# Second MoE from its second group of tokens on: seven half-size products and their sums in place of eight

## The chip, the cores and the metric

The kernel runs on one core of a Trainium2 chip. The core has five engines that run side by side, each with its own queue of instructions, taken in order: PE (TensorE, the matrix products), DVE (VectorE), ACT (ScalarE), POOL (GpSimd) and SP, which issues most transfers. The metric is the device time of one execution in microseconds (us), as the median of several runs; lower is better.

## The reference, cut to what matters

```python
attn_out = _attn_ref(**attn_kwargs)              # 4 x 8 heads, 576 positions, 64 wide
x = ...reshape(B * S, H * D)                     # 2304 tokens x 512
x = _moe_ref(x=x, **moe_kwargs)                  # first MoE: 512 -> 1024 -> 512
return _moe2_ref(x=x, **moe2_kwargs)             # second MoE

def _moe2_ref(x, w_gate, w_val, w_out):          # 512 -> 1536 -> 512
    gate = 1.0 / (1.0 + np.exp(-(x @ w_gate)))
    val = x @ w_val
    return (gate * val @ w_out).astype(np.float32)
```

The change is in the two products `x @ w_gate` and `x @ w_val` alone.

## The kernel before

Every float32 or float64 operand is held as two float16 parts, a high part and the remainder (low). A product of two such operands is three products on PE: high by high, high by low, low by high, summed in float32 in PSUM, the memory that PE writes. It has eight banks of 512 float32 columns.

The kernel first does the attention with the first MoE beside it. The first MoE's result, scaled and split in two parts, goes to a scratch in HBM (`x2_d`, 18 blocks of 128 tokens). The second MoE then takes the tokens in five groups: groups 0 to 3 of 512 tokens (four blocks), group 4 of 256.

For a group, the loop `for j in range(12)` makes 128 columns of the hidden 1536 at a time (L1134): 12 matmuls for the gate and 12 for the value, each 128 x 128 weights by 512 token columns (256 in group 4). Then ACT takes the sigmoid (L1139), DVE multiplies it by the value (L1140), ACT rounds the result to float16 (L1142) and DVE makes the low part (L1143). After that comes the product with `w_out`, called `ops` (L1150): 36 matmuls of 512 columns for each block of 128 tokens, and ACT takes the result out (L1154).

The weights of the second MoE come in as float64 words. The list `units` holds their preparation in 76 steps: `w2_dec` makes a float32 of them (`decode`, L166 on ACT, then L167, L168, L171 on DVE), `w2_scale` and `w2_scale_out` work out scales, `w2_split` cuts a piece into the two parts in `split_w`: POOL scales it (L639), ACT rounds it (L642), POOL subtracts (L643). The steps that are left when the second MoE begins are taken during group 0, some for each `j`; the last are `w2_scale_out`, a chain of small DVE instructions that ends with the scale `S_O` (L1066), and the twelve pieces of `w_out`, which POOL can only begin once `S_O` is there.

The order on each engine is not that of the code: a scheduler that reckons with expected durations sets it when the program is built. On the chip each engine then takes its instructions in that fixed order, so one that waits holds up all behind it.

Of the kernel before, what the change touches and what calls it, by code (L numbers as in the profile page):

```python
# [86 lines left out]
def attn_moe_kernel(  # L87
# [45 lines left out]

    def pow2(st, cols, dst, sdst, p=None):
# [914 lines left out]
    def w2_scale(jc):  # L1049
        pow2(w2st, [(4 * jc, 4 * jc + 4)], sw[:, jc, P_G:P_G + 1], sw[:, jc, S_G:S_G + 1], psx[0])  # L1050
# [5 lines left out]
        root2(mx, 1, sw[:, jc, P_L:P_L + 1], sw[:, jc, S_L:S_L + 1])  # L1056
        dve.scalar_tensor_tensor(out=sw[:, jc, W_CG:W_CG + 1], in0=col(P_F), scalar=2.0 ** -23,
                                 in1=sw[:, jc, P_G:P_G + 1], op0=ALU.mult, op1=ALU.mult)
# [51 lines left out]
    grow("gv", NGV, ctx, "left")  # L1110
    ob_p = enter(ctx, "ob", 2)
    for g in range(5):
        n = 4 if g < 4 else 2
# [4 lines left out]
        gvs = []
        for j in range(12):
# [18 lines left out]
            sg = ring("sg", [128, 512], F32)
            act.activation(out=sg[:, 0:nn], in_=prods[0], func=ACTF.Sigmoid, scale=sw[:, j // 4, W_CG:W_CG + 1])  # L1139
            dve.scalar_tensor_tensor(out=sg[:, 0:nn], in0=prods[1], scalar=2.0 ** -16, in1=sg[:, 0:nn],  # L1140
                                     op0=ALU.mult, op1=ALU.mult)
            act.activation(out=gv[:, 0, jj, 0:nn], in_=sg[:, 0:nn], func=ACTF.Copy)  # L1142
            dve.tensor_tensor(out=gv[:, 1, jj, 0:nn], in0=sg[:, 0:nn], in1=gv[:, 0, jj, 0:nn], op=ALU.subtract)  # L1143
# [88 lines left out]
```

## Time and profile before

| what | value |
|---|---|
| median of 3 runs | 1145.22 us (1144.88 to 1147.71) |
| span of the profiled execution, first to last instruction | 1146.8 us |
| PE busy | 990.4 us, 86% of the span |
| DVE busy | 721.4 us, 63% |
| ACT busy | 561.8 us, 49% |
| POOL busy | 405.2 us, 35% |
| mean granted TensorE clock | 0.882 of full speed |

A span is cut into slices or windows, and each engine's busy time in one is given. Busy shares are means over stages with different limits, so they are read stage by stage. The span stands in for the profiled execution's time; it lies within the three runs.

### The profile page before, as it was taken

The numbers are of one execution on the slowest core, as the hardware profiler recorded it, in microseconds if no ns is written. First come the engines' busy times: TensorE is split into PE (matmuls) and PEld (weight loads), VectorE is DVE, ScalarE is ACT, GpSimd is POOL, SyncE is SP. The second block draws the span as 40 slices with busy tenths as digits, with TensorE's granted clock in tenths as the row PEclk, the third lists the DMA queues.
The fourth block names the chain that finished last, engine by engine and source line by source line (L and its number), as shares of the span: only waits on it lengthen the run. The fifth ranks groups of instructions, "written<-read, shape, count | busy, mean of one in ns | idle before, by whom it ended". The sixth has DMA issues, their size and how long they took to land.

```text
span 1146.8 us, 21879 instructions
## 1 busy us (share of the span) xinstructions
PE 990.4 (86%) x8686; PEld 584.7 (51%) x8686; DVE 721.4 (63%) x1537; ACT 561.8 (49%) x1072; POOL 405.2 (35%) x349
## 2 busy tenths in 40 slices
PE   3535665877999889999999989879999999999998
PEld 3433343544555565666677666434444444444475
DVE  7899999799679788967965798892022022022021
ACT  5856567643567565746664567664222122122122
POOL 2556546632355553653555076646100000000000
PEclk9555565565988899999999999999999999999999
DMA  9879999785899998999987523551001100100000
GB/s 303 281 166 252 196 213 246 170 186 149 214 191 192 211 194 221 174 175 232 201 150 162 169 102 129 188 180 37 38 1 37 37 1 2 45 10 1 19 20 19
DMA packets 287863, 158.03 MB, mean 138 GB/s; under 512 B 233104, under 2 KB 258064, under 8 KB 287760
## 3 DMA queue, kind: packets, MB, share of 16 engines
q1 hardware_dynamic: 286736, 155.58, 57.2%
q8 instruction: 68, 1.11, 0.4%
q0 software_dynamic: 1024, 1.05, 0.3%
q14 instruction: 35, 0.29, 0.1%
HBM read 81.75 MB, written 20.05 MB: 89 GB/s over the span
## 4 chain that ended last, share of the span: by engine, by line
PE 42%; DVE 8%; DMA 5%; issue 2%; ACT 2%; POOL 1%; SPq 0%; ACTq 0%; POOLq 0%; DVEq 0%
PE s_ps L1134 20%; PE ops L1150 12%; PE xps L572 2%; PE x2ps L765 2%; DVE w2f L168 2%; DMA pt<-p 2%; PE hps L706 2%; DMA wraw<-in_moe_w_gate_dram 1%; DVE w2f L171 1%; DVE w2f L167 1%; DVE e L731 1%; DMA wraw<-in_moe_w_out_dram 1%; DMA wraw<-in_moe_w_val_dram 1%; PE s_ps L492 1%; POOL p L549 1%
## 5 line engine op out<-in xcount | busy, mean ns | idle before, releaser
L1134 PE MATMUL s_ps<-xb,w2f 128*128 128x512 f16 (+1 forms) x1440 | 291.3, 360 | 8.9 <-DVE sg L1140 5.3
L1134 PEld LDWEIGHTS <-w2f 128*128 128x128 f16 x1440 | 141.4, 99 | 152.0 <-issue 12.4
L549 POOL TENSOR_TENSOR p<-p,p 128x1024 f16<-128x1024 f32 x72 | 158.2, 2197 | 129.7 <-ACT p L548 87.1
L1140 DVE SCALAR_TENSOR_TENSOR sg<-s_ps,sg 128x512 f32<-128x512 f32 (+1 forms) x60 | 38.2, 637 | 261.2 <-ACT sg L1139 261.1
L537 ACT ACTIVATE p<-p,m,sc 128x576 f32<-128x576 f32 x144 | 123.4, 859 | 74.3 <-DVE m L535 66.4
L572 PE MATMUL xps<-gk,pt 128*128 128x64 f16 (+1 forms) x2240 | 132.8, 207 | 15.2 <-DVE xt L628 6.4
L1150 PE MATMUL ops<-w2f,gv 128*128 128x512 f16 x648 | 144.3, 379 | 0.0
L765 PE MATMUL x2ps<-lt,w1f 128*128 128x128 f16 x1728 | 124.7, 222 | 10.1 <-DVE lt L754 7.2
L572 PEld LDWEIGHTS <-pt 128*128 128x128 f16 (+1 forms) x2240 | 106.6, 108 | 45.8 <-issue 20.5
L765 PEld LDWEIGHTS <-w1f 128*128 128x128 f16 x1728 | 105.7, 99 | 30.5 <-issue 19.1
L530 DVE CUSTOM_DVE_ANT_0 p<-s_ps,gk 128x576 f32<-128x576 f32 x144 | 106.2, 750 | 22.8 <-PE s_ps L492 12.9
L1139 ACT ACTIVATE sg<-s_ps,sw 128x512 f32<-128x512 f32 (+1 forms) x60 | 38.5, 642 | 140.4 <-PE s_ps L1134 140.4
L398 PEld LDWEIGHTS <-mask 128*128 128x128 f16 (+1 forms) x1312 | 68.5, 126 | 73.9 <-DVE gb L423 23.8
L1150 PEld LDWEIGHTS <-gv 128*128 128x128 f16 x648 | 63.4, 98 | 75.2
L489 PE MATMUL s_ps<-gk,qt 128*128 128x288 f16 x256 | 61.9, 326 | 28.6 <-DVE m L530 20.0
L398 PE MATMUL bp<-rhs,mask 128*128 128x64 f16 (+1 forms) x960 | 56.5, 234 | 32.7 <-DVE gb L423 22.3
L706 PE MATMUL hps<-w1f,xt 128*128 128x512 f16 x312 | 77.2, 395 | 0.0
L548 ACT ACTIVATE p<-p 128x1152 f16<-128x1152 f32 x54 | 62.4, 1156 | 24.2 <-DMA pt<-p 23.6
L492 PE MATMUL s_ps<-gk,qt 64*128 64x288 f16 x256 | 63.5, 327 | 0.0
L1154 ACT ACTIVATE ob<-ops,sc 128x512 f32<-128x512 f32 x18 | 12.3, 688 | 97.2 <-PE ops L1150 95.7
L1143 DVE TENSOR_TENSOR gv<-sg,gv 128x512 f16<-128x512 f32 (+1 forms) x60 | 38.7, 646 | 32.8 <-ACT gv L1142 32.8
L706 PEld LDWEIGHTS <-xt 128*128 128x128 f16 x384 | 36.9, 101 | 42.5 <-issue 8.1
(164 smaller groups left out, 1477.0 us busy)
## 6 DMA issues: line engine op xcount, KB each, us to landing
gk<-bias_d SPq DMA_DIRECT2D x24, 576.0 KB, 5.7
wraw<-in_moe_w_out_dram SPq DMA_DIRECT2D x20, 512.0 KB, 4.2
wraw<-in_moe_w_gate_dram SPq DMA_DIRECT2D x12, 512.0 KB, 4.0
wraw<-in_moe_w_val_dram SPq DMA_DIRECT2D x12, 512.0 KB, 4.0
sraw<-in_q_dram SPq DMA_DIRECT2D x12, 384.0 KB, 5.1
sraw<-in_k_dram SPq DMA_DIRECT2D x12, 384.0 KB, 4.1
sraw<-in_v_dram SPq DMA_DIRECT2D x12, 384.0 KB, 4.1
bias_d<-gk SPq DMA_DIRECT2D x8, 576.0 KB, 4.5
```

The source lines that it names most:

```text
L398: pe.matmul(big[0:np_, jj // 8, o:o + 64], lhsT, rhs[i].rearrange("p c h g -> p (c h g)"), start=(i == 0), stop=(i == 1),)
L489: pe.matmul(s_[:, n, 0:288], qt[:, 2 * hh + r, :], kt[:, o], start=True, stop=False)
L492: pe.matmul(s_[:, n, 0:288], qt[rows, 4 + r, :], kt[rows, o], start=False, stop=True)
L530: dve.tensor_tensor_reduce(out=pp[:, r].rearrange("p (i j) -> p i j", i=2), in0=ss[r][:, :, 0:288], in1=bi.rearrange("p (i j) -> p i j", i ...
L537: act.activation(out=pp[:, r], in_=pp[:, r], func=ACTF.Exp, bias=m[:, 2 + r:3 + r], scale=col(C), accum_out=sm[:, cs[r]:cs[r] + 1])
L548: act.activation(out=hi, in_=pp, func=ACTF.Copy)
L549: pool.tensor_tensor(out=p16[:, :, 640:1152], in0=pp[:, :, 0:512], in1=hi[:, :, 0:512], op=ALU.subtract)
L572: pe.matmul(o, a, b_, start=(n == 0), stop=(n == len(seq) - 1))
L706: pe.matmul(h, xt[:, xl, kk, off:off + 128], win16[:, 2 * kk + n, wl], start=(kk == 0 and xl == 0 and wl == 0), stop=(kk == 3 and xl == 1),)
L765: pe.matmul(ps[:, dc], wout16[:, f, wl, 128 * dc:128 * dc + 128], lt[:, ll, f], start=(n == 0), stop=(n == 23))
L1134: pe.matmul(ps[:, 0:n], w[:, 4 * (j // 4) + c, wl, o:o + 128], xx[:, 0:n, c, xl, :], start=(m == 0), stop=(m == 11))
L1150: pe.matmul(ps, gvs[j // 4][:, gl, j % 4, 128 * tt:128 * tt + 128], w2h16[2][:, j, wl], start=(m == 0), stop=(m == 35))
```

## The change

From group 1 on, the gate and the value product of 512 hidden columns (a chunk `jc`; there are three) are no longer made of eight products of halved operands (2 halves of the 512 inputs, 2 of the hidden columns, 2 of the tokens) but of seven, on sums and differences of the halves (the scheme of Strassen and Winograd). Group 0 stays as it was.

- `w2_sums` makes the sums of weight halves once for each of six matrices (gate and value, three chunks); `x2_sums` makes those of the tokens once for each group. A sum is made in float32 and split in two parts: 14 DVE and 4 ACT instructions for each call.
- `product` is one of the seven: 12 matmuls of 256 token columns (128 in group 4) into a PSUM bank. There are six banks for it, and two for `ops`.
- `seven` adds the seven products up: ACT copies the first one, DVE makes seven additions. `gate_val7` applies sigmoid, product and split to the four quarters that come out.

```diff
+    def add(out_, a, b, op=ALU.add):
+        dve.tensor_tensor(out=out_, in0=a, in1=b, op=op)
+    def split_sum(x, dst):
+        act.activation(out=dst(0), in_=x, func=ACTF.Copy)
+        add(dst(1), x, dst(0), ALU.subtract)
...
+    def w2_sums(mat, jc):
...
+        add(x, a11(0), a21(0), ALU.subtract)
+        add(u, a11(1), a21(1), ALU.subtract)
+        add(x, x, u)
+        split_sum(x, s3)
...
+        split_sum(u, a21)
...
+    def product(w, x, nn):
+        p = ps_b.tile([128, 2, 256], F32, name="prod", tag="prod")
+        for jf in range(2):
+            m = 0
+            for kk in range(2):
+                for (wl, xl) in ((0, 0), (0, 1), (1, 0)):
+                    pe.matmul(p[:, jf, 0:nn], w(wl, kk, jf), x(xl, kk), start=(m == 0), stop=(m == 5))
+                    m += 1
+        return p[:, :, 0:nn]
+    def seven(mat, jc, xs_, nn):
+        w = wsum[mat, jc]
+        a, b, c, d = (f32t()[:, :, 0:nn] for _ in range(4))
+        act.activation(out=a, in_=product(w["a11"], xs_["b11"], nn), func=ACTF.Copy)
+        add(b, product(w["s2"], xs_["t2"], nn), a)
+        add(a, product(w["a12"], xs_["b21"], nn), a)
+        add(c, product(w["s3"], xs_["t3"], nn), b)
+        p5 = product(w["s1"], xs_["t1"], nn)
+        add(b, p5, b)
+        add(d, p5, c)
+        add(c, product(w["a22"], xs_["t4"], nn), c)
+        add(b, product(w["s4"], xs_["b22"], nn), b)
...
+    load_x2(1)
+    gvs = []
+    gate_val(0, 4, xb.pop(0), gvs)
+    while units:
+        units.pop(0)()
...
+    for jc in range(3):
+        for mat in range(2):
+            w2_sums(mat, jc)
+        if jc == 0:
+            xs_ = x2_sums(1)
+    second_out(0, 4, gvs)
...
+    for g in range(1, 5):
+        n = 4 if g < 4 else 2
+        if g < 4:
+            load_x2(g + 1)
+        gvs = []
+        gate_val7(n, xs_, gvs)
+        if g < 4:
+            xs_ = x2_sums(g + 1)
+        second_out(g, n, gvs)
```

Besides, the scales of the gate and value weights are halved, so that sums fit float16, and some buffers get other places. Lines named below in rows of the changed kernel are its own: L1140 is `add`, L1143 the ACT half of `split_sum`, L1210 a matmul of `product`, L1218 the ACT copy in `seven`, L1278 `ops` (L1150 before), L1254 and L1122 the DVE instructions of group 0 (L1140 and L1143 before), L1253 and L1121 their ACT counterparts, L1071 the scale `S_O` (L1066 before), and L1282 ACT's copy of `ops` (L1154 before).

The first place is DVE at the end of the preparation of `w_out`: the small chain `L147` to `L1066` that ends with `S_O`. Before, these rows stand there, with one instruction of group 0 between them:

```order
L147 TENSOR_SCALAR cl<-tot 128x3
L149 TENSOR_SCALAR ci<-cl 128x3
L150 TENSOR_SCALAR ci<-ci 128x3
L151 TENSOR_SCALAR sw<-ci 128x3
L1143 TENSOR_TENSOR gv<-sg,gv 128x512
L153 RECIPROCAL rc<-sw 128x3
L1062 TENSOR_TENSOR sw<-sw 128x3
L1063 TENSOR_REDUCE sc<-sw 128x1
L1064 RECIPROCAL sc<-sc 128x1
L1066 SCALAR_TENSOR_TENSOR sw<-sw,sc 128x1 x3
```

In the changed kernel the end of the same chain (`L1068` to `L1071`) reads as follows, on DVE; `fr` are the float32 buffers, `w2f_...` weights, `w2s_...` split sums of weights, `xb` tokens:

```order
L1254 SCALAR_TENSOR_TENSOR fr<-s_ps,fr 128x512
L1140 TENSOR_TENSOR fr<-xb,fr 128x2x2x128
L1140 TENSOR_TENSOR fr<-xb 128x2x2x128
L1140 TENSOR_TENSOR w2s_11182<-fr,w2s_11182 128x512
L1068 TENSOR_REDUCE sc<-sw 128x1
L1140 TENSOR_TENSOR w2s_11207<-fr,w2s_11207 128x512
L1140 TENSOR_TENSOR fr<-w2f_9501 128x512
L1140 TENSOR_TENSOR fr<-fr,xb 128x2x2x128
L1122 TENSOR_TENSOR gv<-fr,gv 128x512
L1069 RECIPROCAL sc<-sc 128x1
L1140 TENSOR_TENSOR fr<-fr 128x512
L1071 SCALAR_TENSOR_TENSOR sw<-sw,sc 128x1 x3
```

Between the reduction `acc` (L140) that begins the chain and L1071 there stand 33 instructions of 512 elements on DVE in the changed kernel (27 sums and 6 of group 0), and three of group 0 before.

The second place is also on DVE, further on, where the sums end and the first products of group 1 (`prod`) are added:

```order
L1140 TENSOR_TENSOR w2f_9501<-fr,w2f_9501 128x2x256
L1140 TENSOR_TENSOR fr<-fr,w2f_9501 128x512
L1140 TENSOR_TENSOR w2s_11309<-fr,w2s_11309 128x512
L1140 TENSOR_TENSOR w2s_11334<-fr,w2s_11334 128x512
L1140 TENSOR_TENSOR fr<-w2f_9501,fr 128x512
L1140 TENSOR_TENSOR w2s_11334<-fr,w2s_11334 128x512
L1140 TENSOR_TENSOR fr<-prod,fr 128x512
L1140 TENSOR_TENSOR fr<-fr,w2f_9501 128x512
L1140 TENSOR_TENSOR fr<-prod,fr 128x512 x2
L1140 TENSOR_TENSOR w2s_11334<-fr,w2s_11334 128x512
L1140 TENSOR_TENSOR fr<-prod,fr 128x512 x7
```

From L1071 to the first row with `prod` there are 69 sums. All of them, those of the third chunk too, stand ahead of the first addition of a product.

The third place is ACT in the same stretch, where the copies of `ops` of group 0 (L1282) and the first copy of a product (L1218) stand between the ACT halves of the sums:

```order
L1143 ACTIVATE w2s_11284<-fr 128x512
L1282 ACTIVATE ob<-ops,sc 128x512 x3
L1143 ACTIVATE w2s_11284<-fr 128x512
L1143 ACTIVATE w2s_11309<-fr 128x512
L1143 ACTIVATE w2f_9500<-fr 128x2x256
L1282 ACTIVATE ob<-ops,sc 128x512
L1143 ACTIVATE w2s_11309<-fr 128x512
L1143 ACTIVATE w2f_9501<-fr 128x2x256
L1143 ACTIVATE w2s_11309<-fr 128x512
L1143 ACTIVATE w2s_11334<-fr 128x512 x2
L1218 ACTIVATE fr<-prod 128x512
```

Each L1143 waits for a sum on DVE, so the copies behind it come after that sum. On PE, the 144 matmuls of `ops` of group 0 stand in one piece, behind the last product of group 0 and ahead of all products of group 1; before, products of group 1 stood among them.

## Rows read from the trace of the kernel before

**Rows 1.** Page, part 1: busy time, share of the span, instructions of each engine.

```profile
PE 990.4 (86%) x8686; PEld 584.7 (51%) x8686; DVE 721.4 (63%) x1537; ACT 561.8 (49%) x1072; POOL 405.2 (35%) x349
```

**Rows 2.** Busy time in windows: length, engines, then PE clock, DMA share, GB/s.

```profile
764.00:786.00 22.00, 19.84 (x84) 8.68 (x85) 16.27 (x38) 12.37 (x27) 4.27 (x6) 0.92 0.23 73
786.00:823.00 37.00, 37.00 (x173) 16.84 (x172) 2.91 (x4) 10.21 (x17) 19.48 (x21) 1.00 0.14 50
880.00:1000.00 120.00, 120.00 (x558) 54.38 (x556) 18.00 (x26) 21.93 (x33) 0.00 (x0) 1.00 0.09 29
```

**Rows 3.** Chain that ended last: start, us, engine, tile, line, count.

```profile
842.72 10.36 PE s_ps L1134 x48
...
880.27 28.92 PE ops L1150 x134
...
1095.67 7.86 PE s_ps L1134 x72
...
1142.69 0.69 ACT ob L1154
```

**Rows 4.** Timeline of PE, first MoE: products of 128 columns in one run.

```profile
643.10 4.80 PE L765 MATMUL x2ps<-lt,w1f 128*128 128x128 f16 x83
```

**Rows 5.** Timeline of PE, end of group 0's gate and value products.

```profile
780.18 8.79 PE L1134 MATMUL s_ps<-xb,w2f 128*128 128x512 f16 x40
...
790.11 22.83 PE L1150 MATMUL ops<-w2f,gv 128*128 128x512 f16 x105
```

**Rows 6.** Timeline of DVE, group 0: decoding, then the chain to the scale.

```profile
768.92 0.41 DVE L167 TENSOR_SCALAR w2f<-w2f 128x512 int32<-128x512 int32 x1
769.25 0.68 DVE L171 SCALAR_TENSOR_TENSOR w2f<-wraw,w2f 128x512 int32<-128x512 int32 x1
769.85 0.68 DVE L168 SCALAR_TENSOR_TENSOR w2f<-wraw,w2f 128x512 int32<-128x512 int32 x1
770.57 0.69 DVE L171 SCALAR_TENSOR_TENSOR w2f<-wraw,w2f 128x512 int32<-128x512 int32 x1
...
777.31 0.16 DVE L140 TENSOR_REDUCE acc<-w2st 128x1 f32<-128x4 f32 x1 [0.25 <-ACT w2junk L1043]
...
782.96 0.30 DVE L1066 SCALAR_TENSOR_TENSOR sw<-sw,sc 128x1 f32<-128x1 f32 x3
```

**Rows 7.** Timeline of POOL: weight pieces beside a busy DVE, then beside an idle one.

```profile
735.14 3.00 POOL L639 TENSOR_SCALAR w2tmp<-w2f,sw 128x512 f32<-128x512 f32 x2
738.42 3.18 POOL L643 TENSOR_TENSOR w2f<-w2tmp,w2f 128x512 f16<-128x512 f32 x2 [0.27 <-ACT w2f L642]
...
783.29 1.36 POOL L639 TENSOR_SCALAR w2tmp<-w2f,sw 128x512 f32<-128x512 f32 x2 [17.65 <-DVE sw L1066]
784.73 2.27 POOL L643 TENSOR_TENSOR w2f<-w2tmp,w2f 128x512 f16<-128x512 f32 x2
```

**Rows 8.** Timeline of POOL and DVE where both are dense.

```profile
757.24 3.09 POOL L643 TENSOR_TENSOR w2f<-w2tmp,w2f 128x512 f16<-128x512 f32 x2 [1.23 <-ACT w2f L642]
757.66 0.68 DVE L1140 SCALAR_TENSOR_TENSOR sg<-s_ps,sg 128x512 f32<-128x512 f32 x1
...
760.31 2.48 POOL L639 TENSOR_SCALAR w2tmp<-w2f,sw 128x512 f32<-128x512 f32 x2
...
762.76 2.88 POOL L643 TENSOR_TENSOR w2f<-w2tmp,w2f 128x512 f16<-128x512 f32 x2
...
764.66 1.53 DVE L168 SCALAR_TENSOR_TENSOR w2f<-wraw,w2f 128x512 int32<-128x512 int32 x1
...
766.11 0.68 DVE L1140 SCALAR_TENSOR_TENSOR sg<-s_ps,sg 128x512 f32<-128x512 f32 x1
```

**Rows 9.** Groups of instructions from 823 to 1143 us, shapes apart: busy, mean ns.

```profile
L1134 PEld LDWEIGHTS <-w2f 128*128 128x128 f16 x1118 | 109.4, 98 | 102.5
...
L1142 ACT ACTIVATE gv<-sg 128x512 f16<-128x512 f32 x35 | 22.0, 630 | 26.5 <-DVE sg L1140 26.5
...
L1140 DVE SCALAR_TENSOR_TENSOR sg<-s_ps,sg 128x256 f32<-128x256 f32 x12 | 5.1, 425 | 48.8 <-ACT sg L1139 48.8
```

More of the change, by code (lines that the diff above doesn't have):

```diff
@@ L55 @@
 BD1 = 4
-NGV = 2
+NFR = 12
 KLEAD = 16
@@ L154, in root2 @@
         if sdst is not None:
-            dve.tensor_scalar(out=sdst, in0=rc, scalar1=2.0 ** 14, scalar2=None, op0=ALU.mult)
+            dve.tensor_scalar(out=sdst, in0=rc, scalar1=2.0 ** e, scalar2=None, op0=ALU.mult)
         return rc
@@ L1019, in attn_moe_kernel @@
     w2_p = enter(ctx, "w2", 1, "right")
-    w2r_p = enter(ctx, "w2r", 3, "right")
-    w2d_p = enter(ctx, "w2d", 1, "right")
-    w2t_p = enter(ctx, "w2t", 2, "right")
+    grow("xb", 1, ctx)
+    grow("gv", 2, ctx)
+    grow("fr", 2, ctx)
+    d2 = ctx.enter_context(ExitStack())
+    w2r_p = enter(d2, "w2r", 3, "right")
+    w2d_p = enter(d2, "w2d", 1, "right")
+    w2t_p = enter(d2, "w2t", 2, "right")
     w2f = [w2_p.tile([128, 12, 512], F32, name=f"w2f{i}") for i in range(3)]
@@ L1055, in w2_scale @@
         dve.tensor_reduce(out=mx, in_=tot, axis=AX, op=ALU.max)
[L1056 to L1057 removed]
+        root2(mx, 1, sw[:, jc, P_L:P_L + 1], sw[:, jc, S_L:S_L + 1], 13)
+        dve.scalar_tensor_tensor(out=sw[:, jc, W_CG:W_CG + 1], in0=col(P_F), scalar=2.0 ** -21,
                                  in1=sw[:, jc, P_G:P_G + 1], op0=ALU.mult, op1=ALU.mult)
@@ L1101, in load_x2, with f32t, split_gv @@
         xb[g] = t
-    grow("xb", 1, ctx)
-    grow("sg", 2, ctx)
-    grow("gv", 2, ctx)
     load_x2(0)
     glob["s"].close()
+    m1.close()
     grow("xb", 1, ctx, "left")
-    grow("sg", 1, ctx, "left")
-    grow("gv", NGV, ctx, "left")
+    grow("gv", 2, ctx, "left")
+    grow("fr", 3, ctx, "left")
     ob_p = enter(ctx, "ob", 2)
-    for g in range(5):
-        n = 4 if g < 4 else 2
+    def f32t():
+        return ring("fr", [128, 2, 256], F32)
+    def split_gv(y, gv, js, t0, w):
+        hi, lo = (gv[:, l, js, t0:t0 + w] for l in range(2))
+        act.activation(out=hi, in_=y, func=ACTF.Copy)
+        dve.tensor_tensor(out=lo, in0=y, in1=hi, op=ALU.subtract)
@@ new lines, in half_w, with get, half_x @@
+    def half_w(mat, jc, kh, fh):
+        def get(l, kk=None, jf=None):
+            if kk is None:
+                return w2h16[mat][:, 4 * jc + 2 * kh:4 * jc + 2 * kh + 2, l, 256 * fh:256 * fh + 256]
+            return w2h16[mat][:, 4 * jc + 2 * kh + kk, l, 256 * fh + 128 * jf:256 * fh + 128 * jf + 128]
+        return get
+    def half_x(xx, nt, kh, th):
+        def get(l, kk=None):
+            if kk is None:
+                return xx[:, nt * th:nt * th + nt, 2 * kh:2 * kh + 2, l, :]
+            return xx[:, nt * th:nt * th + nt, 2 * kh + kk, l, :]
+        return get
@@ new lines, in add, with part @@
+    def add(out_, a, b, op=ALU.add):
[4 more added lines that the diff above has]
+    def w2_sums(mat, jc):
+        a11, a21, a12, a22 = (half_w(mat, jc, kh, fh) for kh, fh in ((0, 0), (0, 1), (1, 0), (1, 1)))
+        st_ = sw_p.tile([128, 3, 2, 2, 256], F16, name=f"w2s{mat}{jc}")
+        def part(n):
+            return lambda l, kk=None, jf=None: (st_[:, n, l] if kk is None else
+                                                st_[:, n, l, kk, 128 * jf:128 * jf + 128])
+        s2, s3, s4 = (part(n) for n in range(3))
+        u, v, x = f32t(), f32t(), f32t()
+        add(x, a11(0), a21(0), ALU.subtract)
+        add(u, a11(1), a21(1), ALU.subtract)
+        add(x, x, u)
+        split_sum(x, s3)
+        u, x = f32t(), f32t()
+        add(u, a21(0), a22(0))
+        add(x, a21(1), a22(1))
+        add(u, u, x)
+        add(v, u, a11(0), ALU.subtract)
+        add(v, v, a11(1), ALU.subtract)
+        split_sum(v, s2)
+        split_sum(u, a21)
+        x = f32t()
+        add(x, a12(0), v, ALU.subtract)
+        add(x, x, a12(1))
+        split_sum(x, s4)
+        wsum[mat, jc] = dict(a11=a11, a12=a12, a22=a22, s1=a21, s2=s2, s3=s3, s4=s4)
@@ new lines, in x2_sums, with tile_, part @@
+    def x2_sums(g):
+        xx = xb[g]
+        nt = 2 if g < 4 else 1
+        b11, b21, b12, b22 = (half_x(xx, nt, kh, th) for kh, th in ((0, 0), (1, 0), (0, 1), (1, 1)))
+        def tile_():
+            return f32t().rearrange("p k (t q) -> p t k q", q=128)[:, 0:nt]
+        def part(n):
+            t = xs_p.tile([128, 2, 2, 2, 128], F16, name=f"x2s{n}")
+            return lambda l, kk=None: t[:, l, 0:nt] if kk is None else t[:, l, 0:nt, kk]
+        t1, t2, t3, t4 = (part(n) for n in range(4))
+        u, v, x = tile_(), tile_(), tile_()
+        add(u, b12(0), b11(0), ALU.subtract)
+        add(v, b12(1), b11(1), ALU.subtract)
+        add(u, u, v)
+        add(x, b22(0), u, ALU.subtract)
+        add(x, x, b22(1))
+        split_sum(x, t2)
+        y = tile_()
+        add(y, b22(0), b12(0), ALU.subtract)
+        add(v, b22(1), b12(1), ALU.subtract)
+        add(y, y, v)
+        split_sum(y, t3)
+        split_sum(u, t1)
+        y = tile_()
+        add(y, b21(0), x, ALU.subtract)
+        add(y, y, b21(1))
+        split_sum(y, t4)
+        return dict(b11=b11, b21=b21, b22=b22, t1=t1, t2=t2, t3=t3, t4=t4)
@@ L1137, in attn_moe_kernel, with gate_val7, second_out @@
                 prods.append(ps[:, 0:n].rearrange("p t q -> p (t q)"))
[L1138 to L1143, printed above, removed]
+            sg = f32t().rearrange("p j q -> p (j q)")[:, 0:nn]
+            act.activation(out=sg, in_=prods[0], func=ACTF.Sigmoid, scale=sw[:, j // 4, W_CG:W_CG + 1])
+            dve.scalar_tensor_tensor(out=sg, in0=prods[1], scalar=2.0 ** -14, in1=sg, op0=ALU.mult, op1=ALU.mult)
+            split_gv(sg, gv, jj, 0, nn)
+    def gate_val7(n, xs_, gvs):
+        nn = 64 * n
+        for jc in range(3):
+            gv = ring("gv", [128, 2, 4, 512], F16)
+            gvs.append(gv)
+            gates = {}
+            for fh, th, r in seven(0, jc, xs_, nn):
+                act.activation(out=r, in_=r, func=ACTF.Sigmoid, scale=sw[:, jc, W_CG:W_CG + 1])
+                gates[fh, th] = r
+            for fh, th, r in seven(1, jc, xs_, nn):
+                y = gates[fh, th]
+                dve.scalar_tensor_tensor(out=y, in0=r, scalar=2.0 ** -14, in1=y, op0=ALU.mult, op1=ALU.mult)
+                split_gv(y, gv, slice(2 * fh, 2 * fh + 2), nn * th, nn)
+    def second_out(g, n, gvs):
         for tt in range(n):
             i = 4 * g + tt
-            ps = ps_m.tile([128, DM], F32, name="ops", tag="m")
+            ps = ps_o[0].tile([128, DM], F32, name="ops", tag="m")
             m = 0
@@ L1163, in attn_moe_kernel @@
                     sp.dma_start(out=out[r0:r0 + 64, :], in_=ob[64 * par:64 * par + 64])
+    load_x2(1)
[3 more added lines that the diff above has]
+        units.pop(0)()
+    d2.close()
+    grow("fr", NFR - 5, ctx)
+    sw_p = enter(ctx, "w2s", 1, "left")
+    xs_p = enter(ctx, "x2s", 1, "left")
+    ps_o = [ps_m]
+    for jc in range(3):
+        for mat in range(2):
[3 more added lines that the diff above has]
+    second_out(0, 4, gvs)
+    pss.close()
+    ps_b = enter(ctx, "ps_b", 6, space=PSUM)
+    ps_o[0] = enter(ctx, "ps_o", 2, space=PSUM)
+    for g in range(1, 5):
[7 more added lines that the diff above has]
+        second_out(g, n, gvs)
 _INS = ['q', 'k', 'v', 'wb', 'moe_w_in', 'moe_w_out', 'moe_g_ln', 'moe2_w_gate', 'moe2_w_val', 'moe2_w_out']
```

24 lines of the change are left out of this document (12 added, 12 removed).

## The prediction

> **What bounds the kernel now.** Part 1 of the page [rows 1] shows PE busy for 86% of the span, but that is a mean over stages, so the windows come next [rows 2]. From 764 to 786 us DVE is the full engine (16.3 of 22 us, most of it decoding weights) and PE has gaps. From 786 us on PE is busy in every microsecond (37.00 of 37.00, 120.00 of 120.00), DVE in 15% of 880 to 1000 (18.0 of 120), and the clock granted is 1.00, that is 2.4 GHz. The chain that ended last [rows 3] is PE alone from there to 1142.69, where the last ACT copy begins. So from 786 us on a matmul saved is time saved, unless PE has to wait for something new; and DVE, idle there, is the engine that gets the new work.
>
> The same rows give PE's prices: 10.36 us for 48 matmuls of 512 columns is 0.2158 each, and 7.86 for 72 of 256 columns is 0.1092 each. For 128 columns the nearest rows are the first MoE's [rows 4]: 83 in 4.80 us, less about 0.22 for the last one to drain, over 82 steps: 0.0559 each, each with weights of its own, as after the change.
>
> **The change, part by part.**
>
> *Matmuls.* In a full group 288 of 512 columns (62.15 us) become 3 chunks x 2 x 7 x 12 = 504 of 256 (55.04): 7.1 us less in each of three groups. In group 4, 288 of 256 (31.4) become 504 of 128 (28.2): 3.2 less. Together 24.6 us.
>
> *DVE in the steady groups.* A chunk needs 14 additions, 4 products and 4 low parts, 22 instructions. DVE's 512-element ones take 0.68, yet start 0.60 apart, or 0.72 where one waits for the one just before it [rows 6]; few of the sums do, so I take 0.62. That is 13.6 us (15.8 at 0.72) beside 168 x 0.1092 = 18.3 us of PE: hidden. `x2_sums` adds 14 (8.7 us) to about one chunk of a group, which makes 22.3 against 18.3; the 4 us of lag are less than the 7.9 that six banks hold (six products of 12 x 0.1092). In group 4 an instruction of 256 elements takes 0.425 [rows 9], some 0.345 apart, so 7.6 us against 168 x 0.0559 = 9.4. ACT has 10 instructions a chunk at 0.63. All of this costs nothing while PE is the slower; if that cover goes, a chunk costs what DVE exceeds PE by.
>
> *The weight sums.* Six calls of 14 DVE instructions and one call of `x2_sums` are 98 sums. They come when group 0 is ending, and the order rows show where: 27 ahead of L1071 (with 6 of group 0, so 33), 69 behind it, all ahead of the first addition of a product. I walk through it.
>
> (1) The chain to `S_O` begins with L140 at 777.31, as before, since the decoding ahead of it is the same. Before, L1066 was done at 783.26 [rows 6]. Now 33 x 0.62 = 20.5 and eight small ones, 0.8 together (bounded by 0.16 each, as L140), lie in between: 777.5 + 21.3 = 798.8. POOL's twelve pieces of `w_out` began at 783.29 on L1066 [rows 7]; they begin 15.5 us later.
>
> (2) PE ends group 0's products at 780.18 + 24 x 0.2158 = 785.4 (24 of the 40 in [rows 5] are group 0's). `ops` stands next on PE and wants the first piece: 798.8 + 0.68 (half of 1.36) + 0.63 for ACT = 800.1. PE stands for 14.7 us; before, it took products of group 1 and `ops` there [rows 5].
>
> (3) POOL and DVE now work at the same time, and the trace shows that they hinder each other. Beside an idle DVE two pieces take 1.36 + 2.27 = 3.63 us of POOL, beside a busy one 3.00 + 3.18 = 6.18 [rows 7]. DVE pays too: from 757.66 to 766.11 it does eight instructions [rows 8], six at 0.60 and two (L167) at 0.33 [rows 6], 4.26 us by their free pitch, in 8.45. It lost 4.19 beside six POOL instructions that take 5.9 us when free, a factor of 0.71. Twelve pieces are 21.8 us of free POOL time. The bounds are 0 and 21.8 us lost; by the factor 15.5. One of those eight took an operand from PSUM and did not queue, while the sums all read two operands from SBUF, so I take 17.
>
> By the Trainium skill (SBUF — State Buffer, SBUF: two separate sides) GpSimd and a DVE instruction with two SBUF inputs share a port pair as an exclusive lock that the winner holds for its whole instruction. By that rule the loss would be the full 21.8 us and the end 5 us later than mine; the factor of 0.71 in this trace says that part of a POOL instruction is overlapped.
>
> (4) The first addition of a product starts after 69 more sums: 798.8 + 69 x 0.62 + 17 = 858.6.
>
> (5) PE in between: three blocks of `ops` go at POOL's pace, six pairs of 6.18 us, to about 836. The fourth needs a bank, freed by ACT's copy L1282, which stands behind an L1143 that waits for the 39th of the 69 sums: 798.8 + 24.2 + 17 = 840.0, plus 0.63 and 0.69 of ACT and 0.3 of passing on, 841.6. It takes 36 x 0.2158 = 7.8, to 849.4; six products fill the six banks, to 857.3. The seventh needs ACT's L1218, behind an L1143 on the 65th sum: 856.1 + 1.6 = 857.7. Both routes say 858. From there DVE frees a bank each 0.62 to 1.3 us, and PE needs one each 1.31.
>
> (6) What is left at 858: 36 products of group 1, 47.2 us; `ops` of groups 1 to 3, 432 x 0.2158 = 93.2; groups 2 and 3, 110.1; group 4, 28.2 and 72 x 0.2158 = 15.5. Sum 294.2. At group ends the last quarters' low parts are wanted about when they are ready, for which I add 1.5 in all (between 0 and some 6, two a group). PE ends at 1153.7, before at 1142.7: 11.0 later. The same from the other side: PE stands for 858 - 785.4 - 31.1 - 7.9 = 33.6 us and saves 24.6.
>
> The clock: PE's gap of 14.7 us will probably bring some microseconds at 1.2 GHz, as the gaps around 764 to 786 did (0.92 there [rows 2]); it falls where POOL sets the pace, so I count nothing. If it reached the fourth block, it would cost up to 3 us.
>
> The sum is made against the profiled execution, span 1146.8, 1.6 over the median of the three runs: 1157.8 in its terms, 1156.2 as a median.
>
> **The rivals.** *A, DVE and POOL do not hinder each other here.* The sums are of another form than L168 and L171, and with a loss of 0 the same walk gives 841 in place of 858, PE ends at 1136.7 and the median is 1139. It decides from a loss of 6 us down, where PE resumes at 847. For it: 798.8 and the matmul prices stand on firm rows, only the loss is borrowed. Against it: both engines' rows show the loss, on each side. A loss of 2.6 to 9.4 us would leave the time within 0.3%.
>
> *B, the additions hold PE up.* If each waits for the one before it (0.72) and the lag of `x2_sums` is not caught by six banks, the stretch to 858 grows by 102 x 0.1 = 10 us, and up to 4 us a group come on top: 1166 to 1178. For it: a chain of additions on `b` runs through a chunk. Against it: the order puts independent sums between.
>
> *C, weight loads set the pace of 128-column matmuls.* A load takes 0.098 [rows 9]; if not hidden, group 4 takes 504 x 0.098 = 49.4 in place of 28.2: 21 more, 1177. Against it are the 83 matmuls with 83 loads at 0.0559 [rows 4]. The Trainium skill (TensorE: Matmul & The Clock Gate, Back-to-back issue gap) gives some 81 ns for sustained pairs of a load and a matmul of 128 columns, by which group 4 would take 40.8 and the total 12.6 us more, so 1169; the trace's 56 and 216 ns for 128 and 512 columns agree instead with what the page calls the isolated gap.
>
> **How the numbers follow.** The forecast (PE resumes between 852 and 865, 1150 to 1163 us) has 0.60; A with a loss under 2.6 us 0.13; a loss from 2.6 to 9.4 us 0.12; B 0.13; C 0.02. What a measurement of this kernel can tell from no change is about 0.3%, 3.4 us: faster 0.13, within it 0.12, slower 0.75. The predicted time is 1156. The range leaves out A and the upper part of B and C: 1143 to 1170; the forecast's own is 1150 to 1163.
>
> **What the profile after would show.** Right: POOL's first L639 for `w_out` near 799, with a long wait on L1071; PE with a gap of some 15 us from 785 and `ops` of group 0 stretched to about 849; DVE full from 766 to about 860 with L643 near 1.6 and sums of 0.68 mixed with 1.1 to 1.6; the first add with `prod` near 859; PE full behind it, 0.109 and 0.056 a matmul. Wrong: sums that stay at 0.68 beside POOL (A); PE waiting for L1140 in groups 2 and 3 (B); group 4's products at 0.08 or more (C). The prediction also fails if the decoding ahead of 777 ends elsewhere, since all after it moves along.

## The result and the profile after

The changed kernel takes 1157.65 us (median of 4 runs, 1153.35 to 1159.7), the kernel before 1146.0 beside it: a ratio of 1.0099, 95% interval 1.0073 to 1.0124. It is slower by 11.65 us. The profiled execution has a span of 1157.9 us, against 1146.8 before.

The page of the changed kernel, part 1 (the line that answers to [rows 1]), and the windows of the tail (columns as in [rows 2]):

```profile
PE 974.7 (84%) x9550; PEld 655.0 (57%) x9550; DVE 899.6 (78%) x1845; ACT 595.2 (51%) x1136; POOL 419.0 (36%) x349
```

```profile
764.00:786.00 22.00, 19.23 (x82) 8.10 (x81) 21.69 (x38) 13.36 (x27) 5.58 (x4) 0.92 0.21 74
786.00:800.00 14.00, 3.37 (x16) 1.42 (x15) 14.00 (x33) 4.33 (x7) 0.74 (x1) 0.76 0.22 75
800.00:823.00 23.00, 13.67 (x52) 5.62 (x52) 16.86 (x23) 5.75 (x10) 22.85 (x13) 0.70 0.00 0
823.00:842.00 19.00, 13.30 (x58) 5.44 (x56) 14.77 (x17) 8.28 (x15) 15.09 (x12) 1.00 0.00 1
842.00:862.00 20.00, 18.24 (x131) 12.77 (x131) 20.00 (x34) 9.32 (x16) 0.00 (x0) 1.00 0.14 53
880.00:1000.00 120.00, 120.00 (x929) 90.65 (x927) 81.87 (x132) 36.52 (x58) 0.00 (x0) 1.00 0.07 23
```

PE has less to do (974.7 us busy against 990.4) and ends later. Before, it was busy in every microsecond from 786 on [rows 2]; now it does 3.37 us of work in the 14 from 786, 13.67 in the next 23, 13.30 in the next 19. From 851.69 on it has no gap (timeline of PE below).

The timeline of DVE says why (start, length; in brackets the idle time before a row and what ended it):

```profile
778.35 0.16 DVE L140 TENSOR_REDUCE acc<-w2st 128x1 f32<-128x4 f32 x1
...
798.93 0.29 DVE L1071 SCALAR_TENSOR_TENSOR sw<-sw,sc 128x1 f32<-128x1 f32 x3
799.21 0.69 DVE L1140 TENSOR_TENSOR fr<-fr,w2f 128x512 f32<-128x512 f32 x1
...
807.04 0.69 DVE L1140 TENSOR_TENSOR fr<-w2f 128x512 f32<-128x512 f16 x1
813.19 1.23 DVE L1140 TENSOR_TENSOR w2s<-fr,w2s 128x512 f16<-128x512 f32 x1 [5.46 <-ACT w2s L1143]
814.35 1.64 DVE L1140 TENSOR_TENSOR fr<-fr 128x512 f32<-128x512 f32 x1
...
818.13 1.09 DVE L1140 TENSOR_TENSOR fr<-w2f 128x512 f32<-128x512 f16 x1
...
859.63 0.68 DVE L1140 TENSOR_TENSOR fr<-prod,fr 128x512 f32<-128x512 f32 x1
```

`S_O` (L1071) comes at 798.9, 16.0 us later than before [rows 6], and the first addition of a product at 859.63, with the sums of both kinds in between. POOL and PE in the same stretch:

```profile
799.26 9.70 POOL L639 TENSOR_SCALAR w2tmp<-w2f,sw 128x512 f32<-128x512 f32 x2 [29.68 <-DVE sw L1071]
809.03 2.27 POOL L643 TENSOR_TENSOR w2f<-w2tmp,w2f 128x512 f16<-128x512 f32 x2
...
815.42 3.27 POOL L639 TENSOR_SCALAR w2tmp<-w2f,sw 128x512 f32<-128x512 f32 x2
818.65 3.15 POOL L643 TENSOR_TENSOR w2f<-w2tmp,w2f 128x512 f16<-128x512 f32 x2
```

```profile
781.44 7.93 PE L1248 MATMUL s_ps<-xb,w2f 128*128 128x512 f16 x36
809.00 10.96 PE L1278 MATMUL ops<-w2f,gv 128*128 128x512 f16 x39 [19.64 <-ACT w2f L642]
...
836.57 3.40 PE L1278 MATMUL ops<-w2f,gv 128*128 128x512 f16 x15 [1.18 <-POOL w2f L643]
842.93 7.93 PE L1278 MATMUL ops<-w2f,gv 128*128 128x512 f16 x36 [2.96 <-ACT ob L1282]
851.69 1.47 PE L1210 MATMUL prod<-xb,w2f 128*128 128x256 f16 x12 [0.83 <-ACT ob L1282]
...
859.54 1.47 PE L1210 MATMUL prod<-xb,w2s 128*128 128x256 f16 x12
...
1109.98 0.83 PE L1210 MATMUL prod<-xb,w2f 128*128 128x128 f16 x12
...
1138.12 15.70 PE L1278 MATMUL ops<-w2f,gv 128*128 128x512 f16 x72
```

PE stands for 19.64 us until the first piece of `w_out` is cut, then follows POOL, waits for a copy of `ops` on ACT, and runs unbroken from 851.69.

### The profile page after: what moved, and what is told of

It reads as the page before. It is cut to its first block, busy times and chain, and to the rows that moved or that the text cites. A ratio compares the mean times of both kernels' runs of the same rounds, so it can differ in the third digit from the quotient of the medians.

```text
span 1157.9 us, 24060 instructions
## 1 busy us (share of the span) xinstructions
PE 974.7 (84%) x9550; PEld 655.0 (57%) x9550; DVE 899.6 (78%) x1845; ACT 595.2 (51%) x1136; POOL 419.0 (36%) x349
## 4 chain that ended last, share of the span: by engine, by line
PE 38%; DVE 11%; POOL 3%; ACT 3%; DMA 2%; issue 2%; SPq 0%; ACTq 0%; DVEq 0%; POOLq 0%
PE prod L1210 17%; PE ops L1278 10%; PE xps L572 3%; PE x2ps L765 3%; DVE w2f L168 2%; PE hps L706 2%; POOL w2tmp L639 2%; DVE w2f L171 2%; DVE fr L1140 1%; DMA pt<-p 1%; POOL w2f L643 1%; DVE w2f L167 1%; PE s_ps L706 1%; DVE gv L1122 1%; DMA wraw<-in_moe_w_out_dram 1%
## 5 line engine op out<-in xcount | busy, mean ns | idle before, releaser
L1140 DVE TENSOR_TENSOR fr<-prod,fr 128x512 f32<-128x512 f32 (+1 forms) x168 | 101.1, 620 | 108.3 <-PE prod L1210 104.2
L1278 PE MATMUL ops<-w2f,gv 128*128 128x512 f16 x648 | 144.7, 383 | 26.6 <-ACT w2f L642 20.1
L572 PE MATMUL xps<-gk,pt 128*128 128x64 f16 (+1 forms) x2240 | 136.2, 210 | 13.9 <-DVE xt L628 6.1
L765 PE MATMUL x2ps<-lt,w1f 128*128 128x128 f16 x1728 | 128.7, 226 | 9.0 <-DVE mm L717 4.5
L765 PEld LDWEIGHTS <-w1f 128*128 128x128 f16 x1728 | 109.9, 102 | 25.2 <-issue 14.7
L1278 PEld LDWEIGHTS <-gv 128*128 128x128 f16 x648 | 63.9, 99 | 105.1 <-issue 32.4
L1210 PEld LDWEIGHTS <-w2f 128*128 128x128 f16 x1152 | 101.4, 98 | 12.1 <-issue 1.1
L1210 PEld LDWEIGHTS <-w2s 128*128 128x128 f16 x864 | 76.2, 98 | 7.3
L639 POOL TENSOR_SCALAR w2tmp<-w2f,sw 128x512 f32<-128x512 f32 x36 | 47.6, 1331 | 68.1 <-DVE sw L155 38.2
L1121 ACT ACTIVATE gv<-fr 128x512 f16<-128x512 f32 (+1 forms) x60 | 34.6, 586 | 73.0 <-DVE fr L1268 67.3
L1248 PE MATMUL s_ps<-xb,w2f 128*128 128x512 f16 x288 | 67.0, 387 | 4.9 <-DVE fr L1254 3.2
L1210 PE MATMUL prod<-xb,w2f 128*128 128x256 f16 (+1 forms) x576 | 63.4, 259 | 0.8 <-ACT ob L1282 0.8
```

Source lines behind the costliest of these rows:

```text
L572: pe.matmul(o, a, b_, start=(n == 0), stop=(n == len(seq) - 1))
L639: pool.tensor_scalar(out=tmp, in0=w, scalar1=s_, scalar2=0.0, op0=ALU.mult, op1=ALU.add)
L765: pe.matmul(ps[:, dc], wout16[:, f, wl, 128 * dc:128 * dc + 128], lt[:, ll, f], start=(n == 0), stop=(n == 23))
L1140: dve.tensor_tensor(out=out_, in0=a, in1=b, op=op)
L1210: pe.matmul(p[:, jf, 0:nn], w(wl, kk, jf), x(xl, kk), start=(m == 0), stop=(m == 5))
L1248: pe.matmul(ps[:, 0:n], w[:, 4 * (j // 4) + c, wl, o:o + 128], xx[:, 0:n, c, xl, :], start=(m == 0), stop=(m == 11))
```

## The experiments

In the traces the profiled executions reach this stage at different times (an identical order of PE's instructions up to `ops` put its start at 784.32 in one run and 791.84 in another), so stretches are measured from a common row, and the times are medians beside the kernel before on the same chip.

**Fewer sums.** One call of `w2_sums` in place of six:

```
-    for jc in range(3):
-        for mat in range(2):
-            w2_sums(mat, jc)
-        if jc == 0:
-            xs_ = x2_sums(1)
+    w2_sums(0, 0)
+    wsum.update(((mat, jc), wsum[0, 0]) for mat in range(2) for jc in range(3))
+    xs_ = x2_sums(1)
```

> Only the 14 weight sums of chunk 0 of the gate weights are made, and all six places use their result; 70 of the 98 sums ahead of the first addition are left out, so the gate and value products are not those of the reference. Of the 28 that are left (with x2_sums), 28 still stand ahead of the last chain instruction of w2_scale_out, as in the changed kernel, so S_O stays late (799). Theory (DVE's sums behind S_O, and their collision with POOL, set when PE resumes; the late S_O alone does not): POOL cuts w_out alone in some 22 us to 821 to 824, the fourth block of ops ends near 832, products of group 1 begin there and run unbroken; they began at 851.7 in the changed kernel, so the time falls by 17 to 22 us, to 1136 to 1141. Rival (the late S_O and the 20 us gap of PE behind it are the loss): that gap stays, so the time stays within 5 us of 1157. Rival A (no collision): 70 x 0.62 = 43 us of DVE go, but POOL's pace is the same with and without sums, so ops end as in the changed kernel and the time falls by 10 us or less.

Measured: 1141.4 us, ratio 0.9955 (0.9923 to 0.9986). The timelines of DVE, POOL, then PE:

```profile
785.98 0.16 DVE L140 TENSOR_REDUCE acc<-w2st 128x1 f32<-128x4 f32 x1
...
803.61 0.29 DVE L1071 SCALAR_TENSOR_TENSOR sw<-sw,sc 128x1 f32<-128x1 f32 x3
```

```profile
803.93 4.27 POOL L639 TENSOR_SCALAR w2tmp<-w2f,sw 128x512 f32<-128x512 f32 x2 [26.62 <-DVE sw L1071]
...
814.65 1.36 POOL L639 TENSOR_SCALAR w2tmp<-w2f,sw 128x512 f32<-128x512 f32 x2
816.08 2.27 POOL L643 TENSOR_TENSOR w2f<-w2tmp,w2f 128x512 f16<-128x512 f32 x2
```

```profile
841.78 1.47 PE L1210 MATMUL prod<-xb,w2f 128*128 128x256 f16 x12 [0.82 <-ACT ob L1282]
```

`S_O` is still behind 28 instructions of 512 elements (17.6 us after L140, 20.6 in the changed kernel); 23 of them are sums and five are group 0's, where the expectation took all 28 for sums. And yet 16 us are gained, just short of the theory's 17 to 22 and more than either rival allows. POOL, alone, cuts two pieces in 1.36 + 2.27. From L140 (785.98 in this run) to the first product it is 55.8 us, against 73.3 (851.69 - 778.35). The late `S_O` alone is not the loss; what stands behind it is.

**`S_O` first.** All sums are put behind the scale chain, nothing else is moved:

```
+    with tc.issue_after(glob["so"].ins):     # the last instruction of w2_scale_out
         for jc in range(3):
             for mat in range(2):
                 w2_sums(mat, jc)
```

> All 98 sums stand behind w_out's scale chain on DVE, nothing is left out. Theory (DVE has about 100 instructions and the collision to get through before the first addition of a product, whichever comes first): S_O at 783 to 784, POOL's pieces begin there and collide with the sums just as much, ops of group 0 come 10 to 15 us earlier on PE, but the first addition of a product stays at 855 to 860, PE waits there instead, and the time is 1157 within 4 us. Rival (the late S_O is the loss): PE's gap from 789 to 809 shrinks by 15 us and so does the time, to about 1142.

Measured: 1156.9 us, ratio 1.0096 (1.0062 to 1.0131): no gain. Its timelines of DVE, POOL and PE:

```profile
783.51 0.30 DVE L1071 SCALAR_TENSOR_TENSOR sw<-sw,sc 128x1 f32<-128x1 f32 x3
...
859.62 0.68 DVE L1140 TENSOR_TENSOR fr<-prod,fr 128x512 f32<-128x512 f32 x1
```

```profile
802.14 3.26 POOL L639 TENSOR_SCALAR w2tmp<-w2f,sw 128x512 f32<-128x512 f32 x2
805.37 3.14 POOL L643 TENSOR_TENSOR w2f<-w2tmp,w2f 128x512 f16<-128x512 f32 x2
```

```profile
858.49 2.72 PE L1210 MATMUL prod<-xb,w2s 128*128 128x256 f16 x12 [12.35 <-ACT fr L1218]
```

`S_O` is 15.4 us earlier and the first addition at the same 859.6. `ops` of group 0 begins at 789.63, 19.4 us earlier, which is more than expected. PE's gap of 19.64 us is gone from 789, and one of 12.35 stands at 846 in its place. The largest wait in the profile of the changed kernel is therefore not what sets the end: the work that DVE has to finish before the first addition is, the sums and what POOL adds to them.

**Sums by chunk.** Only chunk 0's sums ahead of group 1:

```
+    w2_sums(0, 0)                    # ahead of group 1
+    w2_sums(1, 0)
...
+            for mat in range(2):     # in gate_val7, ahead of each chunk
+                if (mat, jc) not in wsum:
+                    w2_sums(mat, jc)
```

> Only the weight sums of chunk 0 and x2_sums stand ahead of group 1; those of chunks 1 and 2 come just ahead of each chunk's products, between DVE's additions. Nothing is left out. Theory (DVE's amount of work from 777 to the end of group 1 is the bound, not its order): products begin near 834 instead of 852, but a chunk then wants 50 DVE instructions, 31 us, against 18.3 of PE, so PE waits for additions in chunks 0 and 1, some 12 us each, and group 1's products end at 905 to 914 (906.9 in the changed kernel): 1156 to 1164. Rival (what costs is that all sums stand ahead of the first product): the waits are small and the time falls by the 17 us by which the products begin earlier, to about 1140.

Measured: 1161.83 us, ratio 1.0144 (1.0105 to 1.0182). The windows:

```profile
800.00:823.00 23.00, 21.95 (x90) 9.39 (x90) 4.93 (x4) 10.12 (x18) 22.53 (x24) 0.86 0.00 0
823.00:842.00 19.00, 18.18 (x113) 10.79 (x112) 4.59 (x7) 4.51 (x8) 0.16 (x1) 1.00 0.15 56
842.00:862.00 20.00, 17.28 (x142) 13.48 (x139) 17.39 (x29) 6.99 (x11) 0.00 (x0) 1.00 0.00 1
862.00:880.00 18.00, 16.24 (x140) 13.65 (x141) 18.00 (x31) 6.61 (x12) 0.00 (x0) 1.00 0.01 2
880.00:900.00 20.00, 13.82 (x75) 7.73 (x73) 20.00 (x35) 6.63 (x12) 0.00 (x0) 0.79 0.00 0
```

Products begin 16 us earlier, at 835.85; 4.3 us of that are this execution's own, which reaches L140 at 774.02 (778.35 in the changed kernel). DVE is then full from 862 to 900, and PE is not: it waits 13.2 us behind the first product, 8.9 of them with matmuls of `ops` for group 1's `gv`, 4.3 with products. The time is inside the theory's range, but the theory (the amount of work, not its order) is not borne out as it stands: from 800 to 842 DVE is busy for 9.5 us of 42. It waits 13.5 us for ACT's copies of the tokens' sums, then 13.2 for the first products, and the sums of chunks 1 and 2 stand behind both. Spreading the sums in this way does not help; an order that fills the idle stretch was not tried.

**No POOL beside the sums.** ACT alone cuts `w_out`:

```
     def w2_split(mat, jc, c):
+        if mat == 2:
+            ...
+            act.activation(out=tmp, in_=w2f[2][:, i], func=ACTF.Copy, scale=sw[:, jc, S_O:S_O + 1])
+            for l in range(2):
+                act.activation(out=w2h16[2][:, i, l], in_=tmp, func=ACTF.Copy)
+            return
```

> The changed kernel, but the twelve pieces of w_out are cut by ACT alone (one scaled copy, then two copies to f16), with nothing on POOL; the low halves are then copies of the high ones and the output is not the reference's. All 98 sums stay where they are. Theory (DVE loses some 16 us to POOL's pieces, of which 5.5 pass through ACT): S_O still at 799, sums at 0.62 throughout, the first addition of a product at 843 to 847 instead of 859.6, PE resumes there, and the time falls by 12 to 16 us, to 1142 to 1146. Rival (the sums cost what they cost without POOL; the collision only delays POOL): the first addition stays near 858 and the time within 4 us of 1157.

Measured: 1144.68 us, ratio 0.9983 (0.9956 to 1.001), 13.0 less than the changed kernel. DVE:

```profile
797.10 0.29 DVE L1078 SCALAR_TENSOR_TENSOR sw<-sw,sc 128x1 f32<-128x1 f32 x3
...
821.86 0.69 DVE L1147 TENSOR_TENSOR w2f<-fr,w2f 128x512 f16<-128x512 f32 x1 [2.72 <-ACT w2f L1150]
...
844.15 0.68 DVE L1147 TENSOR_TENSOR fr<-prod,fr 128x512 f32<-128x512 f32 x1
```

From `S_O` to the first addition it is 47.0 us, against 60.7 in the changed kernel: POOL's pieces cost 13.7. That is a net figure. ACT has more to do here (36 instructions for the pieces in place of 12), and the 4.7 us for which DVE waits for ACT in this trace (three waits, the longest shown) are inside the 47.0.

**Seven products from group 2.** Group 1 keeps its eight products, and the weight sums are made beside it:

```
+    def sums(j, last):               # called in group 1 behind quarters j = 3, 5, 7, 9, 11
+        with tc.issue_after(last.ins):
+            for m in ((j - 3) // 2, 5):
+                if m < 5 or j == 11:
+                    w2_sums(m % 2, m // 2)
+    gate_val(1, 4, xb.pop(1), gvs, sums)
+    xs_ = x2_sums(2)
+    second_out(1, 4, gvs)
...
-    for g in range(1, 5):
+    for g in range(2, 5):
```

> Group 1 keeps its eight products of whole operands; the weight sums are made on DVE behind the low parts of group 1, two weights' chunk at a time, and the seven products begin with group 2. Nothing is left out. Theory: in group 1 PE has 62 us of products and 31 of ops of its own, DVE needs 84 x 0.62 = 52 us for the weight sums and 9 for x2_sums beside 24 x 0.68, POOL has nothing left to do; PE stays unbroken from 786 on and keeps the saving of groups 2, 3 and 4, 7.1 + 7.1 + 3.2 = 17.4 us: 1128.6 (1126 to 1133). Rival (the sums hold PE up wherever they stand, as group 1's two PSUM banks pass through DVE behind them): 5 to 15 us of waits on s_ps in group 1, 1134 to 1144.

Measured: 1139.06 us, ratio 0.9926 (0.9886 to 0.9965): faster than before, by less than expected. The time lies in the rival's range, but its waits are not there: PE was without a gap from 793 to 1133 but for 0.82 us, so the shortfall could only lie ahead of that. The next run looks there.

**The other edits alone.** Eight products in all groups, no sums, but the pools, rings and scales of the changed kernel:

```
-        gate_val7(n, xs_, gvs)
-        if g < 4:
-            xs_ = x2_sums(g + 1)
+        gate_val(g, n, xb.pop(g), gvs)
```

> The changed kernel with all its pools, rings and scales, but with the eight products of whole operands in all groups and no sums; it computes what the kernel before does. The run from group 2 on came out 8 to 9 us worse than its 17.4 us of saved matmuls, and its trace shows PE some 6 us behind at the end of group 0. Theory (the new places of the pools xb, gv and fr in SBUF change the order and the waits of the weight decoding, and PE comes 4 to 7 us late to the end of group 0): 4 to 8 us over the kernel before, with PE busy in every microsecond from 792 on. Rival (the shortfall comes from the sums beside group 1): within 2 us of the kernel before.

Measured: 1149.21 us, ratio 1.0028 (1.0005 to 1.005), 3.0 us more than before, some below what was expected and above the rival. On PE its order of instructions up to `ops` of group 0 is that of the run from group 2. The timelines of PE, from the end of group 0's products on, in this run and in the run from group 2, and the end of PE in the kernel before:

```profile
784.32 0.81 PE L1278 MATMUL ops<-w2f,gv 128*128 128x512 f16 x3
...
1131.96 10.31 PE L1278 MATMUL ops<-w2f,gv 128*128 128x512 f16 x47
```

```profile
791.84 0.81 PE L1280 MATMUL ops<-w2f,gv 128*128 128x512 f16 x3
...
917.14 1.47 PE L1210 MATMUL prod<-xb,w2f 128*128 128x256 f16 x12 [0.82 <-ACT ob L1284]
...
1117.48 15.70 PE L1280 MATMUL ops<-w2f,gv 128*128 128x512 f16 x72
```

```profile
1132.35 10.31 PE L1150 MATMUL ops<-w2f,gv 128*128 128x512 f16 x47
```

From the end of group 0's products to its own end PE takes 357.9 us with eight products (1142.27 - 784.32) and 341.3 with seven from group 2 (1133.18 - 791.84): 16.6 less, the 17.4 of saved matmuls less 0.82. The kernel before takes 357.9 too (784.71 to 1142.65; the 288 matmuls of group 0 are complete with the 21st of the 40 in the first line of [rows 5]). So PE does not come late to the end of group 0 in this run, against what was expected, and from there on the other edits cost nothing. The 3.0 us of the medians, and the rest of the shortfall of the run from group 2, some 8 us by its ratio, lie ahead of that point, and their cause stays open: these two profiled executions, with the same order on PE, reach it 7.5 us apart, and the runs from group 2 spread from 1131 to 1145.

**The pools at their old places.** As from group 2, with `xb`, `gv` and `fr` allocated where the kernel before has them:

```
-    grow("xb", 1, ctx)               # ahead of the decoding's pools
-    grow("gv", 2, ctx)
-    grow("fr", 2, ctx)
...
+    grow("xb", 1, ctx)               # behind them, ahead of load_x2(0)
+    grow("fr", 2, ctx)
+    grow("gv", 2, ctx)
```

> As the run from group 2 on (sums beside group 1, seven products from group 2), but xb, gv and fr lie in SBUF as in the kernel before, the decoding pools stay open, fr has 8 tiles, and the sums of the tokens use tiles of wraw. Nothing is left out. Theory (the pools' places cost the 6 us): PE ends group 0 within 2 us of the kernel before, and the saving of 17.4 us shows nearly whole: a ratio of 0.984 to 0.988, 1128 to 1133. Rival (the shortfall sits in group 1, or 8 tiles of fr are too few): 1137 or more, with waits for fr tiles on DVE and ACT.

Measured: 1134.83 us, ratio 0.9893 (0.9863 to 0.9923). It lies between the two expectations. PE ends group 0's products at 784.2, but in the run before, without this edit, it did so at 784.3, and the interval overlaps that of the run from group 2: that the pools' places cost time is not shown. The timeline of PE shows two waits, where the run from group 2 had one of 0.82:

```profile
909.76 1.47 PE L1213 MATMUL prod<-xb,w2f 128*128 128x256 f16 x12 [1.14 <-ACT ob L1287]
914.00 0.27 PE L1213 MATMUL prod<-x2s,w2s 128*128 128x256 f16 x1 [2.77 <-ACT x2s L1143]
```

The second is for the sums of the tokens, which stood behind those of chunk 2's weights on DVE. They were put first:

```
             if j == 11:
+                xs_.update(x2_sums(2))
             for m in ((j - 3) // 2, 5):
```

> As the run before with the old pools, but the sums of group 2's tokens stand ahead of the last two weights' sums, not behind them. Nothing is left out. Theory: in that run PE waited 1.1 + 2.8 us at 909 to 914, the second wait on a copy of the tokens' sums, with 28 weight sums ahead of it that the first chunk does not need; it goes, and the time falls by 3 us, to a ratio of 0.985 to 0.988. Rival (the wait moves to the weight sums of chunk 2, which come later now): the same as the run before, 0.989.

Measured: 1129.77 us beside 1145.55, ratio 0.9875 (0.9857 to 0.9893), the fastest version here. Its timeline of PE:

```profile
906.60 1.47 PE L1213 MATMUL prod<-xb,w2f 128*128 128x256 f16 x12 [1.14 <-ACT ob L1287]
...
1106.94 15.70 PE L1283 MATMUL ops<-w2f,gv 128*128 128x512 f16 x72
```

1.14 us of the waits are left, and from the end of group 0's products at 780.98 PE takes 341.7 us (to 1122.64), 16.3 less than before: the saving less 1.14.

## Why the prediction was right

The reason was right, and the experiments show it. That the number came within 1.7 us is in part luck, since several sizes were off in opposite directions.

*The saving.* The matmul prices of [rows 3, 4] held: a dozen of 256 columns each 1.31 us, and the 504 of 128 columns in group 4 in 28.14 (1109.98 to 1138.12), 0.0558 each, against 28.2 worked out. From the seventh product at 859.54 to PE's end at 1153.82 it is 294.3 us, against 294.2 worked out. The 1.5 us added for group ends did not show, and rivals B and C are out: PE has no wait at all in the trace from 860 on, and 0.0558 is far from a load's 0.098. The 81 ns of the Trainium skill (TensorE: Matmul & The Clock Gate, Back-to-back issue gap) do not hold here either; 504 of them would have been 40.8 us.

*Step (1)* had `S_O` done at 798.8; it was done at 799.2. The chain began 1.0 us later than assumed and took 20.9 us in place of 21.5. Its delay is right but, as the run with `S_O` first shows, costs nothing by itself.

*Step (2)* put the end of group 0's products at 785.4 and the first `ops` at 800.1; they came at 789.2 and 809.0. The first number was worked out with 24 of the 40 matmuls in [rows 5]; 21 are group 0's, which gives 784.7, and the profiled execution was 4.5 us later than that. Why is open. The run with the other edits alone has the same order on PE up to there and was at 784.3, the run from group 2 at 791.8, so the place of one execution does not tell what the edit did. The other part is the first L639, which took 9.04 us (last section). It is hidden, since the fourth block of `ops` has to wait until 842.93 anyway, for ACT's copy behind a sum, as step (5) says.

*Step (3)*, the borrowed term, was 17 us with bounds of 0 and 21.8. Its sum was right and its content only by half. From 799.21 to the first addition at 859.63 the 69 sums take 60.4 us, 19.0 more than at a pitch of 0.60 (41.4); the prediction's 17 and its pitch of 0.62 make 18.4. But of the 19.0 only 8.7 are sums that take longer beside POOL. The other 10.3 are five waits of DVE for ACT, which the prediction put at nothing; in the longest, 5.46 us, ACT's copy L1143 stood behind L642, which stood behind POOL. That the two errors cancel is luck. Where DVE has no waits, in the run with `S_O` first, the borrowed factor held: 100 instructions from 783.80 to 859.62 take 75.8 us, 15.8 more than at 0.60, beside 21.8 us of free POOL time, a factor of 0.73 against the 0.71 taken from [rows 8]. By the Trainium skill (SBUF — State Buffer, SBUF: two separate sides) the two engines share a port pair as an exclusive lock, for which the prediction's estimate was the full 21.8 us of loss; that run shows 15.8.

*Steps (4) and (5)* put the first addition at 858.6 and PE's resumption at 858; they came at 859.63 and 859.54. The route over the fourth block of `ops` set it: six products and the seventh follow that block without a further wait, and the copy L1218 that frees the seventh's bank had ended at 858.45. With `S_O` first the other route sets it, PE's wait of 12.35 us for L1218, and PE resumes 1 us earlier. In the changed kernel PE stood for 859.54 - 789.2 - 31.1 - 7.9 = 31.3 us, against 33.6 in the forecast. *Rival A* was out: sums of 1.09 to 1.64 stand beside POOL, and without POOL's pieces the time falls by 13 us. *The clock* was 0.70 from 800 to 823, where POOL set the pace; the fourth block took 7.93 us, its full-speed time. With `S_O` first it took 9.35, so 1.4 us were lost there, inside the prediction's 3, for which it named no row.

*The total.* From the end of group 0's products PE takes 364.6 us in the changed kernel and 357.9 before, 6.7 more: the 31.3 us less the 24.6 saved. The other 4.5 us by which PE ends later lie ahead of that point, where the prediction had nothing; the median of the run with the other edits alone is 3.0 us over the kernel before. The forecast had 9.0 in place of the 6.7, and 1.5 for group ends. Its surplus in the stage made up for what it left out ahead of it.

So the reason holds: DVE has to finish 96 of the 98 sums, and what POOL adds to them, before the first addition of a product, and PE stands longer for this than the 24.6 us of matmuls that are saved. The run with fewer sums (-16 us) and the one without POOL (-13 us) take parts of that price away (differences of medians to the changed kernel). The same work put behind `S_O` gives -1 and, spread over group 1, +4. The weight sums made beside group 1's eight products, where DVE is idle, give -19 with the same places of the pools, and -28 with the old places and the tokens' sums first, though group 1 then saves nothing.

## What to carry to other kernels

Work moved from a full engine to an idle one must be put where that engine is idle: DVE was at 15% in the later groups [rows 2] and full where the sums were issued. A long gap of an engine in the profile is not its loss until what it does afterwards no longer waits: undo the gap's cause alone before explaining the time by it. And before a difference ahead of a stage is laid to an edit, compare executions of one and the same order: here two of them lay 7.5 us apart.

## What the runs showed of the hardware

In the changed kernel POOL's first L639 came at 799.26, when DVE was already issuing sums without a pause, and took 9.04 us, to 808.3; alone it takes 0.68. During it DVE did 14 sums at 0.60, undisturbed, and POOL's instruction ended 0.57 us after the last of them, when DVE had run into a wait. The same stands in two other runs: with fewer sums the first L639 took 3.61 us, with sums by chunk 5.41, and both ended 0.56 us after DVE's last sum ahead of a wait. In the run with `S_O` first, where POOL and the sums began together at 783.8, the two shared from the start: two pairs of POOL's instructions took 3.33 + 2.71 there and 3.26 + 3.14 later (1.36 + 2.27 alone). So POOL's first instruction was held off by a stream of sums that was already running, and at other times the two engines slowed each other; on what it depends was not tried.

After PE's wait of 12.35 us in that run the next twelve matmuls of 256 columns took 2.72 us, in place of 1.47; the clock granted from 858.4 to 861.2 was 0.50, that is 1.2 GHz, and 0.90 in the 1.8 us behind it.
